# Batch 0's first Q/K heads by another DMA path in fp32, cast on chip, and the first two MLP tiles in another PSUM pool

## The chip, the cores and the metric

The kernel runs on one NeuronCore of a Trainium2 chip. The engines are TensorE (PE, with its weight loads as PEld), VectorE (DVE), ScalarE (ACT), GpSimd (POOL) and SyncE (SP). SP and POOL both issue DMAs here. The metric is the time on the device in microseconds, as a median over runs.

## The reference

```
scores = q k^T / sqrt(64), causal window of 64 keys; softmax; x = attn v   (8 batches, 8 heads, 576 x 64)
x: (8, 576, 512), heads side by side
h = x^T U V                              (rank 32, over the sequence)
u = x + h^T
out = u + relu(u w_ch1) w_ch2            (512 -> 2048 -> 512)
```

All inputs and the output are fp32 in HBM; the kernel computes in bf16 with fp32 accumulation.

## The kernel before

The work is ordered by hand: the program's order is each engine's order. The first attention (batch 0) runs alone at the start. From then on the MLP over 4608 tokens runs in nine chunks `c` of 512 tokens, and the pieces of the attention of batch `c + 1` are put into numbered slots between its matmul groups.

K and Q of batches 0 and 1 are loaded "grouped": 96 partitions, each with six consecutive rows of every head. `load_kq(0, True)` is a generator that issues one DMA on POOL for each step, four in all: K and Q of heads 0 to 3, then of heads 4 to 7. These DMAs cast fp32 to bf16 on the way. POOL also builds the identity and the masks (`affine_select`), between these issues, and then issues v of batch 0 and, in `load_rest`, the first MLP weights and batch 1.

While K is on its way TensorE runs idle matmuls (`turn_over(n, cols, rows)`, into a bank that nobody reads). Then comes the list `order`: `K j` transposes a pair of heads of K on TensorE (12 transposes into one PSUM tile) and evicts it to `kt`; `Q j` does the same for Q; `B j` writes the additive mask into a score bank with a matmul against the identity; `S j` adds the scores and takes the exp on ACT. `B` and `S` use the pool `ps_big` (two tiles of two banks); the transposes use `ps_tp` and the first-phase pool under the tag `mm`. Behind some entries one idle matmul of 512 columns is put.

After `S4` follow the five PV tiles of batch 0 (TensorE, then a reciprocal and a multiply on DVE), the transposes of x into the banks `ua`, the low-rank product (`U`, `HT`), and the eviction of the result into `uTc` in four quarters, two on ACT and two on DVE. Then the first-phase PSUM pools are closed, and a pool `ps_mm` of three banks is opened in their place. The first MLP step of chunk 0, `ch1(0, 1)`, computes two tiles of 128 hidden units side by side, as each quarter of `uTc` comes.

Of the kernel before, what the change touches and what calls it, by code (L numbers as in the profile page):

```python
# [12 lines left out]
FP32 = mybir.dt.float32  # L13
# [3 lines left out]
def kernel(  # L17
# [11 lines left out]
    nc = tc.nc  # L29
    B, H, S, D = q.shape  # L30
    DM = H * D
    R = moe_U.shape[1]
    F = moe_w_ch1.shape[1]
    P = nc.NUM_PARTITIONS
    W = 64
    NB = S // W
    HP = H // 2
# [3 lines left out]
    GR = 6  # L41
# [3 lines left out]
    GP = S // GR  # L45
    NFULL = S // P
    CH = 512
# [11 lines left out]
    const = ctx.enter_context(tc.tile_pool(name="const", bufs=1))  # L59
# [5 lines left out]
    ps_big = ctx.enter_context(tc.tile_pool(name="ps_big", bufs=2, space=bass.MemoryType.PSUM))  # L65
    ps_tp = ctx.enter_context(tc.tile_pool(name="ps_tp", bufs=1, space=bass.MemoryType.PSUM))
    first = ExitStack()
    psum = {
        "spare": first.enter_context(tc.tile_pool(name="ps_s0", bufs=1, space=bass.MemoryType.PSUM)),
        "mm": first.enter_context(tc.tile_pool(name="ps_t0", bufs=2, space=bass.MemoryType.PSUM)),  # L70
    }
# [26 lines left out]
    pts = const.tile([P, HP, 2, NB - 1, W], BF16, name="pts")  # L98
    ptl = const.tile([P, HP, 2, W], BF16, name="ptl")

    held = const.tile([1, 1], BF16, name="held")

    loaded = {}


    def load_kq(b, split):
        grouped = b < NGR
        if grouped:
            kb, qb = (
                r[0:GP, :].rearrange("p (h c d) -> p h c d", h=H, c=GR) for r in (kr[b % 2], qr[b % 2])  # L110
            )
        else:
            kb, qb = kn[b % 2], qn[b % 2]
        loaded[b] = (kb, qb)
        if grouped:
            for h0, h1 in ((0, 4), (4, 8)) if split else ((0, H),):
                hs = slice(h0, h1)
                for t, src in ((kb, k), (qb, q)):
                    nc.gpsimd.dma_start(
                        out=t[:, hs, :, :].rearrange("p h c d -> p h (c d)"),  # L120
                        in_=src[b, hs, :, :].rearrange("h (p c) d -> p h (c d)", c=GR),
                    )
                    yield
        else:
            for t in range(NT):
                rows = P if t < NFULL else W
                for dst, src in ((kb, k), (qb, q)):
                    nc.gpsimd.dma_start(  # L128
                        out=dst[0:rows, t, :, :],
                        in_=src[b, :, t * P : t * P + rows, :].rearrange("h p d -> p h d"),  # L130
                    )
                yield
# [26 lines left out]
    def shift_low(b, copy, t):  # L159
        copy(out=vB[b % 2][0:W, t, :, :], in_=vA[b % 2][0:W, t + 1, :, :])  # L160


    kq0 = load_kq(0, True)
    nc.vector.memset(idle[:], 0.0)
    nc.vector.memset(ident[:], 0.0)
    next(kq0)
    next(kq0)
    nc.gpsimd.affine_select(
        out=ident[:],
        in_=ident[:],  # L170
# [4 lines left out]
        channel_multiplier=1,  # L175
    )
    nc.vector.memset(maskA[:, 0, 0:2, :], 1.0)
    next(kq0)
    next(kq0)

    for n, base, step, mult in ((0, 0, 1, -1), (1, -1, -1, 1), (1, W, 1, -1)):
        nc.gpsimd.affine_select(
            out=maskA[:, 0, n, :],
            in_=maskA[:, 0, n, :],
# [17 lines left out]
    for i in range(2):  # L202
# [5 lines left out]
        out=uf[0][:, 0:NFULL, :], in_=moe_U[0 : NFULL * P, :].rearrange("(c p) r -> p c r", p=P)  # L208
# [46 lines left out]
    def uT_of(c):  # L255
        if c not in uT_tiles:
            uT_tiles[c] = uT_pool.tile([P, TPC, NDC, P], BF16, name="uTc")
        return uT_tiles[c]


    def attention(b, spare=False):
        crossbar = b >= NXB
        odd = b % 2
        kb, qb = loaded[b]
# [11 lines left out]
        def tr(src, j, wide=False):  # L276
            if spare and turn[0] % 3 != 0:
                tpb = psum["mm"].tile([P, 2 * CH], BF16, name="tpm", tag="mm")
                tp = tpb[:, 0:S].rearrange("d (c p) -> d c p", c=GR)
            elif wide:  # L280
                tpw = ps_big.tile([P, 2, 2 * CH], BF16, name="tpw", tag="big")
                tp = tpw[:, 0, 0:S].rearrange("d (c p) -> d c p", c=GR)
            else:
                tp = ps_tp.tile([P, GR, GP], BF16, name="tpg", tag="tp")
            turn[0] += 1
            for c in range(GR):
                for g in range(2):
                    nc.tensor.transpose(  # L288
                        tp[g * D : (g + 1) * D, c, :], src[:, 2 * j + g, c, :], ident[0:GP, 0:GP]
                    )  # L290
            return tp.rearrange("d c p -> d p c")

        def place_of(f, j):
            return f[j].rearrange("d (p c) -> d p c", c=GR)

        def TK(j):
            def f():
                copy = nc.vector.tensor_copy if spare and j == 2 else nc.scalar.copy
                copy(out=place_of(kt, j), in_=tr(kb, j))
            return f  # L300

        def TQ(j):
            def f():
                copy = nc.vector.tensor_copy
                copy(out=place_of(qt, j), in_=tr(qb, j, b == 1))  # L305
            return f

# [354 lines left out]
    def mlp(c):  # L662
        uTc = uT_of(c)
        c1 = [None] * NFC

        def ch1(*ids):
            def f():
                ps = {i: psum["mm"].tile([P, CH], FP32, name="psA", tag="mm") for i in ids}
                for dc in range(NDC):
                    for i in ids:  # L670
                        nc.tensor.matmul(  # L671
                            ps[i][:],
                            w1b[:, dc, i * P : (i + 1) * P],
                            uTc[:, :, dc, :],
                            start=(dc == 0),
                            stop=(dc == NDC - 1),
                        )
                for i in ids:
                    c1[i] = c1_pool.tile([P, CH], BF16, name=f"c1_{i}")
                    if i in DVE_RELU.get(c, DVE_RELU_N):  # L680
                        nc.vector.tensor_relu(out=c1[i][:], in_=ps[i][:])  # L681
                    else:
                        nc.scalar.activation(out=c1[i][:], in_=ps[i][:], func=ACT.Relu)  # L683
            return f

        acc = {}

        def ch2(t, quarter):
            def f():
                g = c * TPC + t  # L690
                if quarter == 0:
                    acc[t] = psum["mm"].tile([P, DM], FP32, name="psU", tag="mm")
                for i in range(4 * quarter, 4 * quarter + 4):
                    nc.tensor.matmul(  # L694
                        acc[t][:],
                        c1[i][:, t * P : (t + 1) * P],
                        w2b[:, i, :],
                        start=(i == 0),
                        stop=(i == NFC - 1),
                    )  # L700
                if quarter == 3:
                    osb = out_pool.tile([P, DM], FP32, name="osb")
                    nc.vector.tensor_tensor(  # L703
                        out=osb[:], in0=acc[t][:], in1=u_tiles[g][:], op=ALU.add
                    )
                    nc.sync.dma_start(out=outf[g * P : (g + 1) * P, :], in_=osb[:])
            return f

        ups = [ch1(i) for i in range(NFC)]
        if c == 0:  # L710
            ups[0:2] = [ch1(0, 1), lambda: None]
            return ups + [ch2(t, r) for u in (0, 2) for r in range(4) for t in (u, u + 1)]
        return ups + [ch2(t, r) for t in range(TPC) for r in range(4)]
# [49 lines left out]
    def turn_over(n, cols, rows=P):  # L763
        for _ in range(n):
            nc.tensor.matmul(
                unread[0:rows, 0:cols], idle[:, 0:rows], idle[:, 0:cols], start=True, stop=True
            )


    turn_over(45, 96)  # L770
    turn_over(30, R, R)
    att = {0: attention(0, spare=True)}
    a = att[0]
    nc.vector.tensor_scalar(
        out=maskA[:, 0, 2, :],
# [7 lines left out]
        out=maskB[:, 0:3, :],  # L783
# [7 lines left out]
    def repeat(copy, mask):  # L791
        pair = mask[:, 1:3, :].rearrange("p (o n) w -> p o (n w)", o=1)
        copy(
            out=mask[:, 3:7, :].rearrange("p (o n) w -> p o (n w)", o=2),
            in_=pair.to_broadcast([P, 2, 2 * W]),
        )
        nc.vector.tensor_copy(out=mask[:, 7, :], in_=mask[:, 1, :])

    repeat(nc.scalar.copy, maskB)
    order = "K0 K1 B0 B1 Q0 Q1 S0 S1 K2 K3 B2 Q2 B3 Q3 S2 S3 B4 S4"  # L800
    for what in order.split():
        j = int(what[1])
        if what[0] in "SB":
            a[what[0]][j]()
        else:
            a["T"][2 * j + (what[0] == "Q")]()
        if what == "Q1":
            load_low_rank()
            nc.scalar.copy(out=ub[0][:], in_=uf[0][:])
        if what in ("B1", "Q1", "S1", "B2", "Q3"):  # L810
            turn_over(1, CH)
    load_rest()
    for t in range(NT + 2):
# [115 lines left out]
```

## Time and profile before

| | |
|---|---|
| time, median of 5 runs | 316.8 us (316.4 to 317.65) |
| the profiled execution | 316.8 us, its span 315.1 us |
| TensorE busy | 306.0 us (97%) |
| DVE, ACT, POOL busy | 162.0, 110.8, 99.4 us |
| moved by DMA | 39.34 MB, mean 125 GB/s |

In a row of the timeline the first number is the start, the second the length in microseconds, and `xN` the number of instructions merged; the bracket holds the idle time of the engine before it and what ended that. In a row of groups the numbers behind the bars are the busy time, the mean of one in ns, and the idle time ahead of it. In the windows view each engine has its busy time and its count; then come the granted clock, the DMA share and GB/s. Matmuls overlap, so a matmul's own length is more than its share of the time.

### The profile page before, as it was taken

To read this page: it belongs to the slowest core of one execution; us is meant where nothing else is said; L and a number is where in the kernel's file an instruction comes from. 1 tells how busy PE (TensorE), PEld (TensorE's weight loads), DVE (VectorE), ACT (ScalarE), POOL (GpSimd) and SP (SyncE) were. 2 spreads that over 40 slices of the span, in tenths; PEclk is the share of its full clock that TensorE was granted. 3 is DMA by queue.
4 is the path that set the end of the run, shared out by engine and by line. 5 is a ranking of instruction groups with operands and counts; after the bars stand their busy time and mean duration, and the time that the engine had idled before them with its cause. 6 is when DMAs were issued, how large, how long until landed. Compare 5 with 4: busy or idle time off the path is not lost.

```text
span 315.1 us, 6910 instructions
## 1 busy us (share of the span) xinstructions
PE 306.0 (97%) x2875; PEld 149.2 (47%) x2875; DVE 162.0 (51%) x297; ACT 110.8 (35%) x178; POOL 99.4 (32%) x129
## 2 busy tenths in 40 slices
PE   7889999999999999899999999999999999999995
PEld 6544554544554544454445444544454444444441
DVE  4465467427655953684358445744574343016011
ACT  3575580458127620533043303440345003201500
POOL 8684264379546534353445470000000000000000
PEclk9999999999999999999999999999999999999999
DMA  7999999999999999999999999954100610010011
GB/s 108 160 201 207 199 162 146 145 215 152 123 145 180 151 146 170 174 139 135 169 176 162 175 157 160 125 133 121 69 2 0 150 68 2 33 67 35 0 67 67
DMA packets 152255, 39.34 MB, mean 125 GB/s; under 512 B 140928, under 2 KB 147072, under 8 KB 152224
## 3 DMA queue, kind: packets, MB, share of 16 engines
q0 software_dynamic: 100624, 18.36, 79.5%
q1 hardware_dynamic: 51600, 20.55, 40.5%
q8 instruction: 22, 0.36, 0.5%
q14 instruction: 9, 0.07, 0.1%
HBM read 36.92 MB, written 9.44 MB: 147 GB/s over the span
## 4 chain that ended last, share of the span: by engine, by line
PE 91%; DMA 4%; DVE 3%; ACT 1%; issue 0%; POOLq 0%
PE psA L671 40%; PE psU L694 36%; PE sc L352 3%; PE psv L593 3%; DMA uTc<-un 3%; PE xw L414 2%; DMA kr<-in_k_dram 2%; PE tpg L288 1%; DVE xs L481 1%; PE sc L342 1%; PE tpu L625 1%; PE pshh L513 1%; ACT pts L372 1%; PE tpm L288 1%; PE xr L414 1%
## 5 line engine op out<-in xcount | busy, mean ns | idle before, releaser
L671 PE MATMUL psA<-uTc,w1b 128*128 128x512 bf16 x576 | 130.8, 379 | 1.5 <-DMA uTc<-un 1.0
L694 PE MATMUL psU<-w2b,c 128*128 128x512 bf16 x576 | 131.2, 379 | 0.1
L694 PEld LDWEIGHTS <-c 128*128 128x128 bf16 x576 | 55.6, 98 | 65.6 <-issue 0.8
L671 PEld LDWEIGHTS <-w1b 128*128 128x128 bf16 x576 | 54.1, 98 | 66.1 <-issue 3.5
L683 ACT ACTIVATE c<-psA 128x512 bf16<-128x512 f32 x84 | 50.0, 597 | 89.5 <-PE psA L671 88.5
L703 DVE TENSOR_TENSOR osb<-psU,un 128x512 f32<-128x512 f32 x36 | 24.7, 690 | 75.6 <-PE psU L694 75.3
L681 DVE TENSOR_SCALAR c<-psA 128x512 bf16<-128x512 f32 x60 | 41.3, 688 | 28.4 <-PE psA L671 28.4
L606 DVE TENSOR_TENSOR un<-psv,xs 128x512 bf16<-128x512 f32 (+1 forms) x40 | 25.5, 684 | 22.9 <-PE psv L593 22.8
L137 POOL DMA_DIRECT2D vA<-in_v_dram x32 | 28.6, 902 | 19.2 <-DMA kr<-in_k_dram 4.9
L128 POOL DMA_DIRECT2D qr<-in_q_dram x30 | 25.5, 850 | 23.1 <-DMA vA<-in_v_dram 13.0
L372 ACT ACTIVATE pts<-sc 128x1024 bf16<-128x1024 f32 x32 | 31.3, 1031 | 3.9 <-PE sc L352 3.9
L128 POOL DMA_DIRECT2D kr<-in_k_dram x30 | 25.3, 844 | 22.6 <-DMA vA<-in_v_dram 14.5
L405 ACT ACTIVATE ptl<-low 128x256 bf16<-128x256 f32 x6 | 2.3, 383 | 62.9 <-PE high L352 62.9
L378 DVE TENSOR_TENSOR pts<-pts,maskA 128x1024 bf16<-128x1024 bf16 x28 | 19.1, 681 | 0.2 <-ACT pts L372 0.2
L481 DVE TENSOR_TENSOR xs<-xw,rcw 128x896 bf16<-128x896 f32 x14 | 15.3, 1091 | 0.5
L352 PEld LDWEIGHTS <-kf 64*64 64x64 bf16 x704 | 9.8, 107 | 7.4 <-issue 7.2
L593 PE MATMUL psv<-hh,vrep 128*128 128x512 bf16 x40 | 12.6, 379 | 0.0
L352 PE MATMUL sc<-qf,kf 64*64 64x128 bf16 (+1 forms) x608 | 11.6, 212 | 0.7 <-DVE qf L305 0.5
L414 PEld LDWEIGHTS <-pts 128*64 128x64 bf16 x512 | 9.9, 110 | 4.3 <-issue 3.0
L628 ACT COPY uTc<-tpu 128x512 bf16<-128x512 bf16 x9 | 5.3, 585 | 10.8 <-PE tpu L625 10.8
L414 PE MATMUL xw<-vA,pts 128*64 128x65 bf16 x217 | 8.5, 195 | 0.0
L528 ACT CAST hh<-pshh 128x512 bf16<-128x512 f32 x7 | 4.1, 582 | 12.5 <-PE pshh L521 12.5
(108 smaller groups left out, 166.8 us busy)
## 6 DMA issues: line engine op xcount, KB each, us to landing
out_dram<-osb SPq DMA_DIRECT2D x36, 256.0 KB, 3.8
vA<-in_v_dram POOLq DMA_DIRECT2D x32, 128.0 KB, 13.9
kr<-in_k_dram POOLq DMA_DIRECT2D x24, 128.0 KB, 12.4
qr<-in_q_dram POOLq DMA_DIRECT2D x24, 128.0 KB, 11.9
w2b<-in_moe_w_ch_dram POOLq DMA_DIRECT2D x4, 512.0 KB, 15.2
w1b<-in_moe_w_ch_dram POOLq DMA_DIRECT2D x2, 512.0 KB, 10.8
w1b<-in_moe_w_ch_dram POOLq DMA_DIRECT2D x1, 1024.0 KB, 9.3
kr<-in_k_dram POOLq DMA_DIRECT2D x2, 288.0 KB, 5.5
```

The costliest lines, as they stand in the source:

```text
L128: nc.gpsimd.dma_start(out=dst[0:rows, t, :, :], in_=src[b, :, t * P : t * P + rows, :].rearrange("h p d -> p h d"),)
L137: nc.gpsimd.dma_start(out=va[:, t, :, 0:D], in_=v[b, :, t * P : (t + 1) * P, :].rearrange("h p d -> p h d"),)
L352: nc.tensor.matmul(sc[g][r0 : r0 + W, col * W : (col + n) * W], keys_of(j, u, rs), queries_of(j, blk, n, rs), start=not spare, stop=last o ...
L372: nc.scalar.activation(out=dst, in_=sc[:], func=ACT.Exp, scale=scale)
L414: nc.tensor.matmul(dst, pts[:, h // 2, h % 2, blk, :] if blk < NB - 1 else ptl[:, h // 2, h % 2, :], rhs, start=True, stop=True,)
L593: nc.tensor.matmul(ps[0][:, n, :], vrep[:, off : off + P], hh["sb"][:], start=True, stop=True)
L606: nc.vector.tensor_tensor(out=u_tiles[g][rs, :], in0=ps[0][rs, n, :], in1=x[rs, t, :, :].rearrange("p h d -> p (h d)"), op=ALU.add,)
L671: nc.tensor.matmul(ps[i][:], w1b[:, dc, i * P : (i + 1) * P], uTc[:, :, dc, :], start=(dc == 0), stop=(dc == NDC - 1),)
L681: nc.vector.tensor_relu(out=c1[i][:], in_=ps[i][:])
L683: nc.scalar.activation(out=c1[i][:], in_=ps[i][:], func=ACT.Relu)
L694: nc.tensor.matmul(acc[t][:], c1[i][:, t * P : (t + 1) * P], w2b[:, i, :], start=(i == 0), stop=(i == NFC - 1),)
L703: nc.vector.tensor_tensor(out=osb[:], in0=acc[t][:], in1=u_tiles[g][:], op=ALU.add)
```

## The change

It does four things. First, K and Q of heads 0 to 3 of batch 0 are loaded by two DMAs on SP, in fp32, into two new tiles, ahead of the loads of U; four instructions cast them to bf16, two on DVE and two on ACT. Second, POOL first builds the identity and the masks and then issues K and Q of heads 4 to 7. Third, the idle matmuls at the start become 124 of 32 columns, the list `order` begins with the two mask matmuls, the single idle matmuls stand elsewhere, and two evictions trade engines (K3 to DVE, Q2 to ACT). Fourth, the first two MLP tiles of chunk 0 take one two-bank tile of `ps_big` in place of two tiles of `ps_mm`.

```diff
+    kst = const.tile([GP, HP, GR, D], FP32, name="kst")
+    qst = const.tile([GP, HP, GR, D], FP32, name="qst")
...
-            for h0, h1 in ((0, 4), (4, 8)) if split else ((0, H),):
-                hs = slice(h0, h1)
+            for hs in (slice(HP, H),) if split else (slice(0, H),):
...
     kq0 = load_kq(0, True)
+    for t, src in ((kst, k), (qst, q)):
+        nc.sync.dma_start(
+            out=t[:].rearrange("p h c d -> p h (c d)"),
+            in_=src[0, 0:HP, :, :].rearrange("h (p c) d -> p h (c d)", c=GR),
+        )
     nc.vector.memset(idle[:], 0.0)
     nc.vector.memset(ident[:], 0.0)
-    next(kq0)
-    next(kq0)
     nc.gpsimd.affine_select(
...
     nc.vector.memset(maskA[:, 0, 0:2, :], 1.0)
-    next(kq0)
-    next(kq0)
...
-                copy = nc.vector.tensor_copy if spare and j == 2 else nc.scalar.copy
+                copy = nc.vector.tensor_copy if spare and j >= 2 else nc.scalar.copy
                 copy(out=place_of(kt, j), in_=tr(kb, j))
...
-                copy = nc.vector.tensor_copy
+                copy = nc.scalar.copy if spare and j == 2 else nc.vector.tensor_copy
                 copy(out=place_of(qt, j), in_=tr(qb, j, b == 1))
...
-                ps = {i: psum["mm"].tile([P, CH], FP32, name="psA", tag="mm") for i in ids}
+                if len(ids) == 1:
+                    ps = {ids[0]: psum["mm"].tile([P, CH], FP32, name="psA", tag="mm")}
+                else:
+                    pair = ps_big.tile([P, 2, CH], FP32, name="psA", tag="big")
+                    ps = {i: pair[:, n, :] for n, i in enumerate(ids)}
...
-    turn_over(45, 96)
-    turn_over(30, R, R)
+    turn_over(124, R, R)
...
-    order = "K0 K1 B0 B1 Q0 Q1 S0 S1 K2 K3 B2 Q2 B3 Q3 S2 S3 B4 S4"
+
+    def cast(dst, src, j, copy):
+        hs = slice(2 * j, 2 * j + 2)
+        copy(out=dst[:, hs, :, :], in_=src[:, hs, :, :])
+
+    kb, qb = loaded[0]
+    cast(kb, kst, 0, nc.vector.tensor_copy)
+    cast(kb, kst, 1, nc.scalar.copy)
+    cast(qb, qst, 0, nc.vector.tensor_copy)
+    order = "B0 B1 K0 K1 Q0 Q1 S0 S1 K2 K3 Q2 B2 Q3 B3 S2 S3 B4 S4"
     for what in order.split():
         j = int(what[1])
+        if what == "K1":
+            cast(qb, qst, 1, nc.scalar.copy)
...
-        if what in ("B1", "Q1", "S1", "B2", "Q3"):
+        if what in ("K1", "Q0", "Q1", "K3", "S4"):
             turn_over(1, CH)
```

## The prediction

> **What bounds the kernel now.** I read the page first, then the timeline of 0 to 24 us, the chain of waits, the waits of the later stretch and the landings.
>
> ```profile
> PE 306.0 (97%) x2875; PEld 149.2 (47%) x2875; DVE 162.0 (51%) x297; ACT 110.8 (35%) x178; POOL 99.4 (32%) x129
> L671 PE MATMUL psA<-uTc,w1b 128*128 128x512 bf16 x576 | 130.8, 379 | 1.5 <-DMA uTc<-un 1.0
> L694 PE MATMUL psU<-w2b,c 128*128 128x512 bf16 x576 | 131.2, 379 | 0.1
> ```
>
> From 23.3 us TensorE is the bound: the windows view has it busy 181.2 of the 185 us from 130 to 315. The MLP rows lose 1.5 us and 0.1 us to waits. So the change can only move the start of this dense part (23.27 us), and the end follows one for one, unless a load becomes late. The start:
>
> ```profile
> 1.26 4.51 PE L765 MATMUL unread<-idle 128*128 128x96 bf16 x75 [1.26 <-DVE idle L164]
> 5.30 0.18 DVE L774 TENSOR_SCALAR maskA<-maskA 128x64 bf16<-128x64 bf16 x1 [1.27 <-POOL maskA L182]
> 6.17 0.45 PE L288 MATMUL tpg<-ident,kr 96*64 96x96 bf16 x12 [0.40 <-DMA kr<-in_k_dram]
> 7.99 0.57 PEld L288 LDWEIGHTS <-qr 96*64 96x64 bf16 x24 [0.42 <-DMA qr<-in_q_dram]
> 9.18 0.75 DVE L305 COPY qf<-tpg 128x576 bf16<-128x576 bf16 x1
> 9.98 0.42 PE L352 MATMUL sc<-qf,kf 64*64 64x128 bf16 x18 [0.24 <-DVE vf L215]
> 10.66 0.70 PE L288 MATMUL tpm<-ident,kr 96*64 96x96 bf16 x24
> 13.65 0.42 PE L352 MATMUL sc<-qf,kf 64*64 64x128 bf16 x18
> 14.12 1.94 ACT L372 ACTIVATE pts<-sc 128x1024 bf16<-128x1024 f32 x2 [1.87 <-PE sc L352]
> 16.11 0.45 PE L414 MATMUL xr<-vA,pts 128*64 128x65 bf16 x16 [0.29 <-ACT pts L372]
> 23.27 1.89 PE L671 MATMUL psA<-uTc,w1b 128*128 128x512 bf16 x8 [0.44 <-DVE uTc L580]
> ```
>
> The reader should see four links. K waits for its DMA until 6.17, Q until 7.99. Two Q evictions of 0.76 on DVE then lead to S1 at 9.98. TensorE is full from 10.66 to S2 at 13.65. Two exps of 0.97 lead to the first PV at 16.11. After it DVE paces five tiles (0.85 each), and a last wait of 0.44 stands before the first MLP matmul.
>
> **The change, part by part.**
>
> *Idle turns.* 45 turns of 96 columns and 30 of 32 become 124 of 32. Single records show 80 ns from start to start for the 96-column turns until 4.68 us, when the granted clock goes from half to full, and 25 ns for the 32-column ones after it. 32 columns at half clock are 80 x 32/96 = 27 ns: 124 end at 1.26 + 3.3 + 0.2 = 4.8. [...] The windows view:
>
> ```profile
> 34.80:42.86 8.06, 8.06 (x201) 4.85 (x200) 5.34 (x8) 6.61 (x11) 2.92 (x4) 1.00 1.76 180
> ```
>
> [...] I take 27 ns. [...]
>
> *Masks.* POOL no longer issues four K/Q DMAs (0.81, 0.68, 0.70, 0.68) ahead of the mask selects; they end near 2.4 instead of 5.25. DVE is then held by its own memsets (last one 3.75 + 0.27), so the row L774 starts at 4.05; maskA 0.18, maskB 0.65, ACT's repeat 0.41: ready at 5.35, before at 6.60. B0 and B1 (4 x 0.216) run 5.35 to 6.22, now before K0.
>
> *Loads.* SP issues K at 0.81 and Q about 0.5 later, ahead of both U loads (needed only by ub at about 8). Fixed time: a lone 256 KB store lands in 2.0 us, at slices of 228 GB/s with DMA 6 tenths busy, so near 375 GB/s when active: 0.7 moving, 1.3 fixed. 576 KB fp32 are then 1.6 us each. K lands at 0.81 + 1.3 + 1.6 = 3.7 at best; the first software K needed 4.8 us from issue for the same source bytes, so 5.6 at worst; I take 4.5. Q: 5.3 to 7.3 in an undisturbed hardware queue; I take 6.2. POOL's two remaining DMAs (heads 4 to 7) are issued at 2.4 and 3.2 instead of 3.15 and 3.84, v from 3.9 instead of 5.25, so no later work on POOL's queue is delayed by its issue. [...] I take 6.2, since both hardware loads are queued over a microsecond before the first software one can move, and keep 8.0 as a rival.
>
> *Casts.* Four of 96x768. ACT: its rows CAST 32x576 0.668 and 128x160 0.338 give 0.79 ns an element, so 0.82. DVE: at one element a cycle (0.69 for 512, 1.09 for 896) 0.96; at the speed of the copy vB<-vA 64x520, 0.28, it would be 0.4. The source is fp32 in SBUF, between the two: 0.55. [...]
>
> *Path to S1.* DVE casts K at 5.1 to 5.65 and Q at 6.2 to 6.75. ACT: K cast 5.35 to 6.17; K0 eviction (0.64) to 7.2; Q cast to 8.0; K1 eviction to 8.7. What is queued behind the Q cast's wait on ACT is that K1 eviction, and S1 waits for it. TensorE: K0, K1 by 6.75, a turn, Q0 7.0 to 7.3, a turn, Q1 8.05 to 8.35. DVE evicts Q1 at 8.55 to 9.3. S1 starts at 9.3, before 9.98: **-0.68**. Q may land as late as 6.75 free of charge; later than that is paid one for one.
>
> *S1 to first PV.* The turn behind S1 goes (10.33 to 10.65): **-0.31**. K2 to S2 was 2.99 us of TensorE with two turns (0.31, 0.32); now one stands there, and B2, B3 find their banks free: 2.65, **-0.34**. The K2/K3 evictions (DVE 10.1 to 11.6) and Q2's on ACT (behind exp1, to 11.7) are done before S2 (12.35); Q3's on DVE ends at 12.55 before S3 (12.75). S2 to PV stays 2.46; the new turn behind S4 hides under the last exp. First PV: 16.11 - 1.33 = 14.8. Heads 4 to 7 landed at 9.48 (K) and 11.09 (Q); they need to be there at 9.7 and 10.65. With the stream starting 0.6 earlier (SP at 0.81 against POOL at 1.36) and shorter hardware transfers it moves by about 1.2: 8.3 and 9.9. Without that, up to 0.4 is lost.
>
> *MLP pair.* psA of tiles 0 and 1 moves from the new three-bank pool, whose first weight load waits for DVE's last release, to the two-bank pool, free since the last xs (21.02). The first matmul then needs only uTc's first quarter (ACT 22.22 + 0.58 = 22.80) while the last HT matmul ends its stream at 22.83; the other quarters are ready at 23.12, 23.29 and 23.72, used at 23.26, 23.69 and 24.1. **-0.44**, at least -0.3. The second psv now needs both relus of the pair (done about 1.1 us after the pair, needed 1.3 after): free.
>
> *What is late next.* The v of batch 1:
>
> ```profile
> PEld L414 <- DMA vA<-in_v_dram: 0.4, 1, 0.4
> 44.39 2.29 ACT L157 COPY vB<-vA 64x520 bf16<-64x520 bf16 x4
> 46.06 0.29 DVE L160 COPY vB<-vA 64x520 bf16<-64x520 bf16 x1 [0.68 <-DMA vA<-in_v_dram]
> ```
>
> Its last tile lands at 46.04, ACT's copy of it ends at 46.68, and PV uses it from about 47.1: slack 0.45. TensorE moves by 1.33 + 0.44 = 1.77, the loads by about 1.2: 1.77 - 1.2 - 0.45 leaves **+0.1** of stall, 0.7 if the loads move by 0.6. A second place is the 1.0 us wait for uTc at 126.4; the stream runs dry several times before it and so follows TensorE again: +0 to +0.3, against up to -1.0 if the collision goes away.
>
> Sum: -0.68 - 0.31 - 0.34 - 0.44 + 0.1 + 0.15 = -1.5. The profiled execution took 316.8 (span 315.1 and 1.7 around it), the same as the median of the five runs. **315.3 us.**
>
> **The rivals.**
>
> *A: Q is served behind the software K.* It lands near 8.0 and S1 slips by 1.25: -1.5 + 1.25 = -0.25, 316.5. [...] A slow DVE cast (0.96) adds 0.4 to the same chain. Around Q at 8.3 the whole gain is gone.
>
> *B, slower: the narrow turns do not open the clock.* In the trace the full clock comes 3.42 us after the first 96-column turn; no 32-column turn ever ran at half clock. The 124 also end at 4.8, just past 4.68, and nothing follows until 5.35. If they do not count, TensorE is at half speed from 5.35 for at least 3.4 us: mask matmuls 0.87 more, 24 transposes 0.65, turn 0.2; partly hidden, net about -0.2 for the kernel. If the gaps between the pieces keep it at half until about 14 us, the full stretch K2 to S2 costs 2.65 more and S3 and the mask 0.7 more: 316.8 - 1.5 + 0.5 + 3.3 = 319.1. It decides once the clock opens later than about 10.5 us. For it: only a quarter of the columns work. Against: they leave TensorE no pause for 3.3 us.
>
> *C: the gain is lost downstream.* The loads don't move, v of batch 1 and uTc each take 0.6 more: 316.8 - 0.7 = 316.1.
>
> **How the numbers follow.** 0.3% of the time is 0.95 us, about what a measurement of this kernel can tell from no change. Main case 0.56 (own range 314.6 to 315.8), A 0.18 (315.9 to 317.0), C 0.11 (315.6 to 316.5), B 0.15 (316.6 to 319.1). Faster: 0.55 of the main case and 0.04 of A and C; slower: 0.12 of B and 0.02 of A; the rest, 0.27, is no change. The range 314.4 to 317.4 leaves out most of B and the ends of the main case.
>
> **What would show it.** Right: turns ending near 4.8 and the clock at full by about 4.7; mask matmuls at 5.3; Q casts before 6.8; S1 near 9.3, first PV near 14.8, first psA near 21.5 with no idle ahead of it. Wrong: 128x512 mask matmuls spaced at 0.43 (B), DVE's Q cast starting at 8 (A), or PV of batch 1 and the wait near 125 us growing (C).

## The result, and the profile after

The changed kernel takes 318.56 us (median of 26 runs, 316.99 to 321.16), the kernel before 316.63 us in the runs beside it (47 runs, 315.6 to 318.72): a ratio of 1.0065, with a 95% interval of 1.005 to 1.008. It is slower by about 1.9 us. The profiled execution took 318.72 us, its span is 317.0 (before 316.8 and 315.1). Three of the medians below include one run in a slower state, which the ratios leave out.

The start in the timeline of the changed kernel, of the same operations as shown of before:

```profile
1.26 3.49 PE L770 MATMUL unread<-idle 128*32 128x32 bf16 x124 [1.26 <-DVE idle L170]
...
5.70 1.86 PE L343 MATMUL sc<-maskB,ident 128*128 128x512 bf16 x4 [0.95 <-DVE maskB L801]
...
6.37 0.56 DVE L807 CAST kr<-kst 96x768 bf16<-96x768 f32 x1 [0.82 <-DMA kst<-in_k_dram]
...
7.50 0.69 PE L289 MATMUL tpg<-ident,kr 96*64 96x96 bf16 x12
...
8.91 0.56 DVE L807 CAST qr<-qst 96x768 bf16<-96x768 f32 x1 [1.98 <-DMA qst<-in_q_dram]
...
9.52 0.69 PE L289 MATMUL tpm<-ident,qr 96*64 96x96 bf16 x12 [0.32 <-DVE qr L807]
...
11.85 1.07 PE L353 MATMUL sc<-qf,kf 64*64 64x128 bf16 x36
...
12.85 0.86 PE L289 MATMUL tpm<-ident,kr 96*64 96x96 bf16 x24
...
15.79 0.81 PE L353 MATMUL sc<-qf,kf 64*64 64x128 bf16 x36
...
18.25 0.45 PE L415 MATMUL xr<-vA,pts 128*64 128x65 bf16 x16
...
19.66 0.22 PE L415 MATMUL xr<-vB,pts 128*64 128x65 bf16 x1 [0.51 <-issue]
...
26.59 1.67 PE L676 MATMUL psA<-uTc,w1b 128*128 128x512 bf16 x7
```

The mask matmuls before, at full clock:

```profile
6.81 1.04 PE L342 MATMUL sc<-maskB,ident 128*128 128x512 bf16 x4
```

Three things are to be seen. The turns end at 4.75, but four mask matmuls take 1.86 us and twelve transposes 0.69, where they took 1.04 and 0.45 at full clock: TensorE is at half speed (a 128x512 matmul takes 0.61 us at 8.60, as at 21.22, where the recorded clock is 0.50, and 0.39 at 13.64, where it is 1.00). DVE waits for K until 6.37 and 1.98 us more for Q, until 8.91. And in the PV tiles stands a pause of 0.51 us that waits for nothing the profile shows ("issue"). The first psA matmul is at 26.59 (23.27 before), without the idle time of 0.44 ahead of it.

The windows view of the changed kernel, in steps of 3.41 us that end at the recorded changes of the clock (columns: stretch, sum, busy time of PE, PEld, DVE, ACT and POOL with their counts, granted clock, DMA share, GB/s). Ahead of the first record, at 13.23, the view prints 1.00 although the matmuls run at half speed:

```profile
2.99:6.40 3.41, 2.46 (x69) 1.94 (x65) 2.48 (x8) 0.43 (x2) 3.41 (x6) 1.00 1.09 247
6.40:9.81 3.41, 3.09 (x36) 1.52 (x36) 1.08 (x2) 2.34 (x4) 2.46 (x4) 1.00 1.34 199
9.81:13.23 3.42, 3.42 (x72) 2.19 (x68) 1.51 (x3) 1.38 (x3) 0.75 (x1) 1.00 2.43 160
...
16.64:20.05 3.41, 2.14 (x52) 1.28 (x51) 1.00 (x3) 3.38 (x6) 2.01 (x4) 1.00 1.21 206
20.05:23.47 3.42, 3.42 (x44) 1.86 (x44) 2.60 (x6) 1.70 (x3) 3.36 (x6) 0.50 1.12 198
```

The clock opens at 13.23 instead of 4.68, after the first step in which TensorE is busy throughout. It closes again at 20.05 for one step, behind a step with only 2.14 us of work. The page shows it as the 7 in its third slice, and the group of the first MLP matmuls has lost its waits:

```profile
PEclk9979999999999999999999999999999999999999
...
L676 PE MATMUL psA<-uTc,w1b 128*128 128x512 bf16 x576 | 130.8, 379 | 0.0
```

Before, that group lost 1.5 us: 0.44 ahead of the first psA and 1.0 for uTc near 126 us. Both waits are gone. The first stood ahead of the dense part. The second stood inside it, and mainly because it is gone the kernel ends only 2.03 us later on TensorE although its dense part starts 3.32 us later.

### The profile page after: what moved, and what is told of

The parts are those of the page before. It is cut to its first block, busy times and chain, and to the rows that moved or that the text cites. A ratio compares the mean times of both kernels' runs of the same rounds, so it can differ in the third digit from the quotient of the medians.

```text
span 317.0 us, 7011 instructions
## 1 busy us (share of the span) xinstructions
PE 309.1 (98%) x2924; PEld 150.2 (47%) x2924; DVE 163.7 (52%) x299; ACT 112.4 (35%) x180; POOL 97.7 (31%) x127
## 4 chain that ended last, share of the span: by engine, by line
PE 93%; DMA 2%; DVE 2%; ACT 1%; issue 0%; SPq 0%
PE psA L676 40%; PE psU L699 38%; PE sc L353 3%; PE psv L594 3%; DMA qst<-in_q_dram 2%; PE xw L415 2%; PE tpg L289 1%; PE xr L415 1%; DVE xs L482 1%; PE tpu L626 1%; PE pshh L514 1%; ACT pts L373 1%; PE tpm L289 1%; PE psh L514 1%; PE unread L770 0%; DVE osb L708 0%
```

## The experiments

A time is the median of a kernel's runs; the ratio is to the kernel before on the same chip, with its 95% interval. "Mean clock" is the granted clock of a run from its first record on; one half-clock step of 3.41 us makes it about 0.995, and a late first opening doesn't show in it. In the changed kernel 22 of 27 runs have 0.995 or less, of before none of 35 in the first set of runs below. "Cover" is the time over which the opening turns keep TensorE busy.

**Turns as before, in the changed kernel.**

```diff
-    turn_over(124, R, R)
+    turn_over(45, 96)
+    turn_over(30, R, R)
```

> The changed kernel with the idle turns of before (45 of 96 columns with 128-column weights, 30 of 32). Theory 'clock' (the 124 narrow turns do not open the clock, and half speed until 13 us is the larger part of the loss): full clock by about 5 us, Q's cast still near 8.9, S1 near 11.7, first PV near 17.2, first psA near 24.0, time 316.2 to 317.2. Theory 'loads' (the late fp32 Q sets the start whatever the clock): first psA stays above 26, time near 318.5.

Measured: 317.01 us (12 runs), ratio 1.0016 [0.999, 1.0043], the mean clock at 0.995 or less in one run. The profiled clock opens at 6.69; S1 is at 11.42, the first PV at 17.42, the first psA at 24.16, close to what 'clock' said. So the turns carry some 1.5 of the 1.9 us; what is left of the change brings no gain.

**Narrow turns alone, in the kernel before** (the same edit the other way).

> The kernel before with only its idle turns exchanged for 124 of 32 columns. Theory 'clock': half clock well past 8 us, first psA 1 to 3 us after 23.3, time 317.5 to 319.5 and a wider spread over runs. Theory 'loads': the turns are harmless, first psA at 23.3, time 316.6.

Measured: 317.8 us (12 runs), ratio 1.0035 [1.0011, 1.0059]; 7 of 12 runs at 0.995 or less. Its windows and waits (engine and line, what it waited for, total, times, longest):

```profile
1.09:4.51 3.42, 3.25 (x122) 3.25 (x122) 2.38 (x16) 1.00 (x1) 3.08 (x5) 1.00 0.55 69
4.51:7.92 3.41, 1.81 (x38) 1.09 (x34) 1.01 (x3) 1.47 (x4) 3.34 (x8) 1.00 1.28 194
14.75:18.16 3.41, 1.54 (x54) 1.14 (x47) 0.90 (x2) 3.39 (x6) 1.55 (x3) 1.00 1.30 199
```

```profile
PE xr L414 <- issue: 1.4, 1, 1.4
```

Here the narrow turns did open the clock, at 4.51: a step happened to lie almost wholly on them. What hurt was another thing: a pause of 1.4 us that waits for nothing, in the PV tiles, after which the clock was half from 18.16 to 24.99 and the first psA came at 27.08. So the time is the one that 'clock' expected, but not by its cause. (The profiled run, 319.3, is the slowest of the twelve.)

**PSUM pair alone, in the kernel before.**

```diff
+                    pair = ps_big.tile([P, 2, CH], FP32, name="psA", tag="big")
+                    ps = {i: pair[:, n, :] for n, i in enumerate(ids)}
```

> The kernel before with only the first two MLP tiles in one PSUM pair. By the prediction's step the wait of 0.44 ahead of the first psA goes and all later work follows: 316.2. If the 1.0 us wait for uTc near 126 us depends on when TensorE arrives there, the time may not follow: 316.6, with that wait at 1.4.

Measured: 316.82 us (12 runs), ratio 1.0015 [0.9989, 1.0041]. First PV to first psA is 6.74 us instead of 7.16, so the 0.42 is won there; at PV of batch 1, near 47 us, 0.3 of it is given back. The wait view of this kernel has a new row for v of batch 1:

```profile
PE xw L414 <- DVE vB L160: 0.3, 1, 0.3
```

**Order, evictions and pair, loads and opening turns as before.**

```diff
-    order = "K0 K1 B0 B1 Q0 Q1 S0 S1 K2 K3 B2 Q2 B3 Q3 S2 S3 B4 S4"
+    order = "K0 K1 B0 B1 Q0 Q1 S0 S1 K2 K3 Q2 B2 Q3 B3 S2 S3 B4 S4"
...
-        if what in ("B1", "Q1", "S1", "B2", "Q3"):
+        if what in ("B1", "Q1", "K3", "S4"):
```

> The kernel before with the pair, the two evictions that trade engines, the order K2 K3 Q2 B2 Q3 B3 and the single idle turns behind B1, Q1, K3 and S4; loads and first turns as before. By the prediction's steps S1 to K2 loses 0.31 and K2 to S2 0.34, first PV near 15.5, first psA near 22.2, time 315.6. If these steps were mis-sized, S2 stays near 13.6 and the time is that of the pair alone.

Measured: 316.08 us (12 runs), ratio 0.9975 [0.9951, 1.0]. S1 to K2 is 0.35 us (0.68 before), K2 to S2 2.78 (2.99), the first PV at 15.54 (16.11). So the trace shows the steps that were expected, while the time is lower by 0.6 us, at the edge of its interval. From first PV to first psA it takes 7.44 us instead of the 6.74 of the pair alone: the fourth PV tile waits 0.35 us for POOL's copy of v of batch 0, and the first psA comes at 22.98, not at 22.2.

**165 narrow turns, in the changed kernel:** `turn_over(165, R, R)`, which last to about 5.7.

> The changed kernel with 165 turns of 32 columns instead of 124, so that they reach to about 5.7 us, where the mask matmuls begin. Theory 'cover' (the clock opens after a window of about 3.4 us of nearly unbroken work, and the 124 turns end 0.95 us before the next matmul): full clock by 4.7 to 8.1 us, and the time of the changed kernel with the wide turns, near 317.0, with few runs whose mean clock is below 0.996. Theory 'narrow' (turns that use 32 of 128 columns count too little): half clock past 9 us and 318 or more, with most runs below 0.996.

Measured: 319.9 us (6 runs), ratio 1.0077 [1.0053, 1.0102]; all six runs at 0.995 or less. The clock opened at 4.48 and was half again from 11.31 to 24.96. Longer cover with narrow turns doesn't help. I read this first as a sign against narrow turns as such. In the profile the clock closes behind a step (7.90 to 11.31) with 1.85 us of work, in which TensorE waits 1.40 us for Q; a pause that waits for nothing, as in the kernel before with narrow turns, does not stand in it.

**The two fp32 loads on POOL's queue, in the changed kernel with the turns of before:** `nc.gpsimd.dma_start` in place of `nc.sync.dma_start`.

> The changed kernel with the wide turns, and the two fp32 loads issued by POOL ahead of its masks instead of by SP, still fp32 to fp32. Theory 'fp32 writes' (the transfer is slow because fp32 rows are written): K and Q move at the 230 to 250 GB/s of the changed kernel and Q lands near 9.4. Theory 'hardware queue' (that queue is the slow one): they move at the rate of the software casts (about 400 GB/s of source) and Q lands near 7.6.

Measured: 319.45 us (one run). K and Q land 5.9 and 7.6 us after issue (5.5 and 7.6 on SP). What moves, by the DMA view: first this kernel from 5.0 to 7.7 us, then the changed kernel from 4 to 7, then the kernel before, with its cast in the transfer, from 5 to 8.

```profile
DMA packets 224, 0.60 MB, mean 222 GB/s; under 512 B 96, under 2 KB 96, under 8 KB 224
```

```profile
DMA packets 721, 0.68 MB, mean 226 GB/s; under 512 B 288, under 2 KB 721, under 8 KB 721
```

```profile
DMA packets 825, 0.56 MB, mean 187 GB/s; under 512 B 106, under 2 KB 825, under 8 KB 825
```

The bytes are those written (K of four heads counts 576 KB as an fp32 load, 288 KB with the cast). In these stretches the fp32 loads move at 222 to 226 GB/s on either queue; the casting loads write 187 GB/s of bf16, which is 374 GB/s of their source. At these rates 576 KB of fp32 take 2.6 us (590 KB / 226), while the same heads cast on the way take 1.6 (295 KB / 187). By this run it is the kind of transfer, not the queue, that makes Q late. The 226 is what these stages show, not a fixed rate of fp32 loads: the next kernel has a short stretch at 378.

**Only K in fp32 by SP; Q of heads 0 to 3 by POOL with the cast, ahead of the masks; turns of before.**

```diff
-    for t, src in ((kst, k), (qst, q)):
+    for t, src in ((kst, k),):
...
+            if split:
+                nc.gpsimd.dma_start(
+                    out=qb[:, 0:HP, :, :].rearrange("p h c d -> p h (c d)"),
+                    in_=q[b, 0:HP, :, :].rearrange("h (p c) d -> p h (c d)", c=GR),
+                )
...
-    cast(qb, qst, 0, nc.vector.tensor_copy)
...
-        if what == "K1":
-            cast(qb, qst, 1, nc.scalar.copy)
```

> The changed kernel with the wide turns, K of heads 0 to 3 alone by SP in fp32, and Q of heads 0 to 3 by POOL with the cast on the way, ahead of the masks; no Q cast. If the loads are the rest of the loss: Q lands near 7.0 instead of 8.9, S1 near 9.3, first PV near 14.9, time near 315.5. If the two queues slow each other down, Q lands after 8 and the time stays near 316.5 to 317.

Measured: 314.93 us (6 runs), ratio 0.9916 [0.9896, 0.9936]. It beats both kernels. Its timeline:

```profile
5.46 0.56 DVE L814 CAST kr<-kst 96x768 bf16<-96x768 f32 x1 [0.67 <-DMA kst<-in_k_dram]
...
7.78 0.45 PE L295 MATMUL tpm<-ident,qr 96*64 96x96 bf16 x12
...
9.78 0.42 PE L359 MATMUL sc<-qf,kf 64*64 64x128 bf16 x18 [0.18 <-DVE vf L222]
```

K is there at 5.46 and Q's transposes run at 7.78 without a wait; S1 is at 9.78, the first PV at 15.37, the first psA at 22.20. K comes 0.9 us earlier than in the changed kernel (6.37), although it is the same fp32 load on the same queue; here no second one follows it. For half a microsecond it moves at 378 GB/s:

```profile
3.00:3.50 0.50, 0.50 (x10) 0.50 (x8) 0.50 (x3) 0.00 (x0) 0.50 (x2) 1.00 1.09 378
```

Why the rate then falls no run here shows.

Run again on another chip it took 315.52 us (10 runs), ratio 0.9948 [0.9924, 0.9972]:

> The version with early loads unchanged (314.93 in its first six runs), to compare on the same chip: 314.6 to 315.4 under every theory.

**Q1's eviction by ACT as well, in the order-and-pair kernel:** `j in (1, 2)` in place of `j == 2`.

> The kernel with the pair and the new order on the old loads (e4_order_pair), with Q1 evicted by ACT instead of DVE. If the two Q evictions behind each other on DVE set S1, S1 moves from 9.95 to about 9.4 and the time from 316.1 to about 315.6. If batch 1's v or uTc near 126 us take it back, the time stays at 316.1.

Measured: 317.41 us (12 runs), ratio 0.9995 [0.9967, 1.0023]: no gain. S1 comes at 9.76 instead of 9.95, but a wait of 0.72 us follows at 11.2 before Q2's transposes.

**Short cover from wide turns, in the changed kernel:** `turn_over(43, 96)`, ending near 4.8.

> The changed kernel with its 124 turns of 32 columns replaced by 43 of 96 columns on a full 128-column weight tile (43 x 80 ns = 3.44 us, ending at about 4.7 as the narrow ones do). Theory 'cover': the clock opens and closes in steps of 3.41 us by how much of such a step TensorE is busy, and turns of 3.5 us seldom fill one: as the changed kernel, 318.5 (318.0 to 319.5), a mean granted clock of 0.995 or less in more than half of the runs. Theory 'width': turns of 32 columns count too little: as the wide turns that last to 5.66, 317.0 (316.6 to 317.4), the clock at 0.997 or more in most runs.

Measured: 318.48 us (10 runs), ratio 1.0064 [1.0043, 1.0085], as the changed kernel; 5 of 10 runs at 0.995 or less, where 'cover' expected more than half. A short cover costs by itself as much as the narrow turns did, and width is not needed to explain it. In the profiled run the clock opened at 4.63 and closed behind a step with 2.08 us of work.

**Long cover on a quarter of the array, 56 turns:** `turn_over(56, 96, R)`.

> The changed kernel with 56 turns of 96 moving columns on a weight tile of only 32 columns (56 x 80 ns = 4.5 us, ending at about 5.75): long cover, a quarter of the array. Theory 'cover': as the wide turns, 317.0 (316.6 to 317.5), the clock at 0.997 or more in most runs. Theory 'width' in the form that the share of the array counts: as the 165 narrow turns, 319 to 320, the clock at 0.995 or less in most runs. 317.0 with the 165 narrow turns at 319.9 would mean that it is the short moving side that counts too little.

Measured: 319.96 us (6 runs), ratio 1.01 [1.0069, 1.013]; all six at 0.995 or less. That was the number of 'width'. Its trace, however, has pauses of the same kind:

```profile
PE sc L353 <- issue: 2.5, 2, 1.4
```

**124 narrow turns where K and Q are early** (the version of 314.93).

> K of heads 0 to 3 by SP in fp32, Q of heads 0 to 3 by POOL with the cast in the transfer (314.9 with the wide turns), now with the changed kernel's 124 narrow turns. If the narrow turns hurt only because K and Q come late behind them: 315.0 to 315.6, the clock at 0.997 or more in most runs. If the turns by themselves hold the clock down whatever follows ('width', or 'cover' with the 0.6 us between 4.75 and the mask matmuls): 316.4 to 317.5, the clock at 0.995 or less in half of the runs or more.

Measured: 317.0 us (10 runs), ratio 0.999 [0.996, 1.0021]; 7 of 10 at 0.995 or less. By the ratios the narrow turns cost 1.3 to 2.3 us here too, with a pause of 1.9 us in the PV tiles that waits for nothing.

**The wait for Q filled, in the kernel with 165 narrow turns:** six 128x512 turns instead of one behind K1.

> The changed kernel with 165 narrow turns (319.9) and six 128x512 turns instead of one behind K1, which fill most of the 1.4 us in which TensorE waits for Q (7.9 to 9.3; the six end at about 8.9). If the clock closes again because of that wait: 317.0 to 317.6, the clock at 0.997 or more in most runs. If it closes because of the narrow turns before it: 319 or more, the clock at 0.995 or less in most runs.

Measured: 321.12 us (4 runs), ratio 1.0128 [1.0072, 1.0184]. Filling the wait did not help (319.9 without; the intervals of the ratios overlap), which is the number of the narrow turns. But in the profile the clock does stay full over the filled wait, from 4.60 to 18.25, so the run does not clear that wait. What is new is that TensorE pauses 0.55 us after 222 matmuls and 1.65 us after 348, again for nothing, and the clock closes in the second of these pauses.

These places gave the third theory. In the profiles with a long pause of this kind in the start it falls after 220 or 222 matmuls or after 347 to 351; the second pause of the row of 56 turns above, 1.14 us, falls after 600. These places are 128 matmuls apart, or close to a multiple of it (some records are missing); each matmul has a weight load (2924 of each on the page of the changed kernel), so 128 are 256 instructions. A transfer on the instruction queue is of 16 KB (23 of them, 0.38 MB, on that page); that one brings 256 instructions, 64 bytes each, is my estimate from these counts. And each such pause ends 1.4 to 1.8 us after such a transfer has ended: in the changed kernel the transfer runs from 17.34 to 18.30 and TensorE resumes at 19.66. The DMA view of the changed kernel from 17.3 to 18.4:

```profile
q0 software_dynamic: 204, 0.20, 110.1%
q1 hardware_dynamic: 17, 0.02, 8.3%
q8 instruction: 1, 0.02, 5.4%
```

The theory, 'refill', is that in these pauses, 0.5 to 1.9 us long, TensorE waits for the next block of its instructions; the traces show the times, not the cause. The runs that follow change the count of turns with the length of cover kept.

**124 turns, cover as long as before, K and Q early.**

```diff
-    turn_over(45, 96)
-    turn_over(30, R, R)
+    turn_over(20, 96)
+    turn_over(104, R, R)
```

> The version with early loads (K by SP in fp32, Q by POOL with the cast, 45 wide turns of 96 columns and 30 narrow ones: 314.9) with 20 turns of 96 columns and 104 narrow ones: the cover ends at 5.65 as before, but there are 124 turns instead of 75. Theory 'refill': TensorE reaches the 350th matmul at about 16.4, before its block of instructions is there (about 18.3): a pause of 1 to 2 us in the first PV tiles, ended by no wait, 316.2 to 317.6, the clock at 0.995 or less in many runs. Theory 'cover': as with 75 turns, 314.9 (314.6 to 315.3). Theory 'width': 315.5 to 316.5 without that pause.

Measured: 317.36 us (10 runs), against 315.52 for the same version with 75 turns on the same chip: 1.8 us for 49 more turns that run in the shadow of the loads. 9 of 10 runs are at 0.995 or less, with 75 turns 1 of 10. The timeline, the windows and, from 15.6 to 16.8, the DMA queues of this kernel:

```profile
16.37 0.19 PE L421 MATMUL xr<-vA,pts 128*64 128x65 bf16 x1
18.16 0.22 PE L421 MATMUL xr<-vB,pts 128*64 128x65 bf16 x1 [1.60 <-issue]
```

```profile
16.59:20.00 3.41, 1.84 (x41) 1.17 (x41) 1.96 (x5) 2.57 (x5) 3.35 (x6) 1.00 1.23 199
20.00:23.41 3.41, 3.41 (x30) 1.56 (x24) 1.97 (x7) 0.00 (x0) 3.41 (x5) 0.50 1.12 211
```

```profile
q8 instruction: 1, 0.02, 5.5%
```

The transfer ends at 16.70 and TensorE resumes 1.46 us later. With 75 turns it ends at 17.51, and the 350th recorded matmul comes only at 19.58, without a pause. The pause also thins the step it falls in to 1.84 us of work, and the clock is half for the next one. This is what 'refill' expected; 'cover' alone (314.9) and 'width' alone (no pause) are not what was seen.

**75 turns on a quarter of the array, K and Q early:** `turn_over(75, 70, R)`.

> The version with early loads with 75 turns of 70 columns on a 32-column weight tile: as many turns and as long a cover (75 x 58 ns = 4.4 us) as its 45 + 30, a quarter of the array. Theories 'refill' and 'cover': 314.9 (314.6 to 315.3), no pause that waits for nothing. Theory 'width': 316 to 317.5, with the clock at 0.995 or less in half of the runs or opening later than 6.5.

Measured: 314.99 us (10 runs), ratio 0.994 [0.9913, 0.9966]; no run at 0.995 or less; the clock opens at 6.53, against 6.84 with wide turns in the run beside it. Width as such costs nothing here.

**The same 75 turns in the changed kernel.**

> The changed kernel with 75 turns of 70 columns on a 32-column weight tile (ends at about 5.65). Theories 'refill' and 'cover': as with 45 wide and 30 narrow turns, 317.0 (316.6 to 317.5), the clock at 0.997 or more in most runs. Theory 'width': 318.5 to 320.

Measured: 318.92 us (10 runs), ratio 1.0062 [1.0029, 1.0096]; 4 of 10 at 0.995 or less. That is the number of 'width', on the late loads only. No pause of the refill kind stands in its first 24 us (one of 0.36 comes near 45.5, and one of 0.5 with the wide turns below); in its profiled run the clock opened at 4.32 and closed at 11.15, over the 1.3 us in which TensorE waits for Q. The profiled run with wide turns below (319.52, one of its two with the clock at 0.995 or less) looks the same: the clock closes over the wait for Q, and the first psA is at 26.14, here at 26.08. So no trace shows why the median is worse than with wide turns; this stays open.

**124 and 75 turns with the same cover, both in the changed kernel, on one chip.**

> The changed kernel with 20 turns of 96 columns and 104 narrow ones: 124 turns as it has, but a cover to 5.65 instead of 4.75. Theory 'refill': the pause at the 350th matmul stays, 318.0 to 319.0 and 0.8 us or more above the same kernel with 75 turns, the clock at 0.995 or less in most runs. Theory 'cover': no more than 0.4 above it, 316.8 to 317.5.

> The changed kernel with the 75 turns of the kernel before (317.01 in its first runs), again on this chip: 316.6 to 317.5 under each theory, the clock at 0.997 or more in most runs, no pause that waits for nothing.

Measured: 318.22 us with 124 (10 runs, ratio 1.0057 [1.0029, 1.0084]), 317.46 with 75 (10 runs, ratio 1.0013 [0.9983, 1.0043]). All ten runs with 124 are at 0.995 or less, 2 of 10 with 75. The waits of the kernel with 124:

```profile
PE tpm L289 <- DVE qr L807: 1.3, 1, 1.3
PE xr L415 <- issue: 1.1, 1, 1.1
```

The first is the wait for Q, in both; the second is the refill. In the profiled run with 75 the clock closed over the first, so late data alone can close it too. The medians differ by 0.76 us, a little under the 0.8 that 'refill' asked for and over the 0.4 of 'cover', but the two intervals overlap.

## Why the prediction was wrong

**The sum, redone with what the traces show** (after minus before). S1 was to move by -0.68 and moved by +2.30 (9.98 to 12.28, the 19th matmul of the row at 11.85); with the wide turns and the clock open it stood at 11.42, so about 1.44 of this is the loads and 0.86 half speed. S1 to K2: -0.31 was said, -0.11 came. K2 to S2: -0.34 said, -0.05 came. S2 to first PV: 0 said, 0 came. First PV to first psA: -0.44 said, +1.18 came. Those make +3.32. Later waits: +0.25 said, -1.29 came (1.0 of it the wait near 126, which is gone). The end of TensorE moves by 3.32 - 1.29 = +2.03, the span by 1.9. The prediction's own sum for C does not come out: -1.5 + 0.6 + 0.6 gives 316.5, not 316.1.

**Loads: the step that failed first.** I took 576 KB at 375 GB/s, worked out from one store, and had Q at 6.2; with both fp32 loads under way 226 GB/s came between 4 and 7 us, and Q's cast starts at 8.91, K's at 6.37. That is 2.2 us past the 6.75 up to which Q was free, and by the prediction's own rule paid one for one: -1.5 + 2.2 = +0.7. The kernel with the wide turns, which keeps this miss without the narrow turns, took 317.01 beside 316.71. Rival A had the direction, but not the cause: the software loads did not get between, they moved 0.02 of the 0.68 MB between 4 and 7 us. Nor does any run show A's 8.0 for Q, an estimate of mine: Q's cast starts at 8.91 here, and Q's transposes at 7.78 where only K is loaded in fp32. With Q taken early and the turns of before, S1 stood at 9.78 and the kernel at 314.9 and 315.5 instead of 317.0 and 317.5. These ran on different chips; by the ratios to the kernel before it is 2 to 3 us for this step. With both steps put right the predicted gain of 1.5 us is reached.

**Turns: right in their spacing, wrong in what they do.** They are 27 ns apart and end at 4.75 (the 201 matmuls in 8.06 us of the prediction's windows row are 40 ns each, with 128x512 ones among them). But I tied the clock to "no pause for 3.3 us" and put the opening at 4.7. The windows show it set in steps of 3.41 us whose phase differs from run to run. In the profile before, a step happened to begin with the first turn (4.68 - 3.41 = 1.27), so that one trace looked like a delay. With the first turn at 1.26 in the others too, the openings at 4.51, 6.69 and 13.23 lie 3.25, 5.43 and 11.97 us behind it, so the steps there don't begin with the turns. 3.49 us of turns lie almost whole in such a step in only a part of the phases: the step with 2.46 us of work did not open the clock, those with 3.25 us (124 narrow turns in the kernel before) and 3.37 us (the 43 wide turns) did. How often the opening is late is not shown: of the four profiled kernels with turns of 3.5 us it was open at 4.51, at 4.63, by 6.06 (124 narrow turns with K and Q early, by the 0.45 us of the transposes there) and, in the changed one, at 13.23. The old turns and the work behind them filled the next step as well (3.01 us of work from 4.68 to 8.09). I had named this as B and given it 0.15, with 319.1 as its time and 10.5 us as the point from which it decides: the opening at 13.23 and 318.56 are its case, but that the two times come so close is luck, since B left out the late loads and the pause. Its reason, that only a quarter of the columns work, is not needed: 43 full-width turns of the same length gave 318.48, and a quarter of the array did no harm with early loads (314.99). With late ones it did (318.92), and that is open. The mask matmuls came at 5.70, not 5.35, because DVE's last copy of the mask took 0.60 us, where the row of before had 0.18; K came later still.

**The count of turns: not in the prediction at all.** 49 more turns are 98 more instructions of TensorE. As the count experiments read, they bring its 350th matmul into the fast part of the PV tiles, before its block of instructions has come. I costed the turns by their time only. In the changed kernel this is 0.51 us of pause and the half-clock step after it, which together with less dense PV work turned -0.44 into +1.18 between first PV and first psA; by 318.22 against 317.46 it is about 0.8 us, with intervals that overlap; on early data it was 1.8. Count and short cover don't add up: the changed kernel has both, and its later arrival shortens the pause to 0.51 from 1.14.

**Right.** The casts took 0.555 on DVE and 0.832 on ACT (0.55 and 0.82 said). The wait of 0.44 ahead of psA went. The order gave -0.33 and -0.21 of the -0.31 and -0.34 when tried on the old loads, though 0.7 us were lost again before the first psA. "What is late next" named the two places that count: with the pair alone, v of batch 1 took 0.3 of the 0.42 back; and the wait near 126 is gone, which is why 3.3 us at the start cost only 2 at the end. That TensorE's late arrival removes it is likely but not shown: with order and pair it was also down to 0.21 us, with the first psA at 22.98.

## What to carry to other kernels

Filler instructions are not free because their engine is idle: here 49 more turns in the shadow of the loads took 1.8 us (317.36 against 315.52), with a wait of 1.6 us on "issue" in the PV tiles. So look for waits on "issue" and for the instruction queue in the profile after changing a count. Check that such a wait is no missing record: 0.47 us in the profile of the 43 wide turns, at 19.59, stands where an idle turn has a weight load and no matmul. To open TensorE's clock at the start, cover clearly more than one of its steps (3.41 us here), since their phase differed from run to run: turns meant to last 4.4 us or more opened it by 6.9 us in every profile here. Keep it open by data that come in time: a wait of 1.3 us in the steps that follow closed it in some profiles. Before a load is split into a plain transfer and a cast on an engine, price it by the bytes that it writes to SBUF, and by what else is under way: by the rates measured here fp32 takes 2.6 us (590 KB at 226 GB/s) where the casting transfer takes 1.6 (295 KB at 187).

## What the hardware showed that was not expected

- TensorE stopped for 0.4 to 1.9 us with no wait that the profile shows ("issue"), after about 222, 350 or 600 matmuls with their weight loads, and resumed 1.4 to 1.8 us after a 16 KB instruction transfer of 1.0 to 1.3 us had ended. That the transfer is the cause is inferred from these times and from the count experiment; no run here moved the transfer itself.
- The clock's steps: in the starts of the profiles, each of the twelve closings came behind a step of 3.41 us with at most 2.14 us of TensorE work. Seven of these steps hold such a pause on "issue", the changed kernel's among them; five hold a wait for K or Q. Two steps with 1.81 and 1.92 us stayed at full, both the first behind an opening, so this is no sharp threshold in busy time. Once closed it needed one to four steps to open again, and a step with over 3 us of work was not always enough (6.40 to 9.81 in the changed kernel).
- With two fp32 loads queued they wrote SBUF at 222 to 226 GB/s on either queue, and the casting loads of the kernel before at 187 GB/s of bf16 from twice as many source bytes. One fp32 load alone reached 378 GB/s for half a microsecond; what lowers the rate is not shown.
